# A decode layer's cached attention: PV in four column tiles, looped batches, part of wo early, and w4 in groups of four rows

## The chip, the cores and the metric

The kernel runs on one core of one Trainium2 chip. The metric is the device time of one execution in microseconds (us), taken as the median of several runs. The profile is one further execution with the hardware profiler on. Its span is just under 2 us shorter than the measured time of the same execution; spans are therefore compared with spans and times with times.

All runs are on a single core, so there is no second die to compare with. A run counts as fast unless it is more than 1.5% above the fastest run of its own kernel.

## The reference

One decode step for 8 sequences. A layer norm, a query projection (`wq`, 4 MB), attention of 32 heads over the last 2048 positions of a cache with 8 key/value head groups, an output projection (`wo`, 4 MB), a residual, then an MLP block whose token-shift branch is identically zero at a sequence length of 1 (so `w1` and `w2` are never read):

```python
def _A_ref(x, k_cache, v_cache, wq, wo):            # B=8, Sq=1, D=512, Hq=32, Hkv=8, Dh=128
    W = min(4096, max(256, Sk // 4))                # Sk = 8192, so W = 2048
    q = (x @ wq).reshape(B, Sq, Hq, Dh).transpose(0, 2, 1, 3)
    k = jnp.repeat(k_cache[:, :, Sk - W:, :], 4, axis=1)
    v = jnp.repeat(v_cache[:, :, Sk - W:, :], 4, axis=1)
    p = softmax(einsum("bhqd,bhkd->bhqk", q, k) * Dh ** -0.5)
    return einsum("bhqk,bhkd->bhqd", p, v).transpose(0, 2, 1, 3).reshape(B, Sq, Hq * Dh) @ wo

# ... B_ref: x1 = x + 0;  x1 + gelu(layernorm(x1) @ w3) @ w4,  F = 1792
h = x + _A_ref(layernorm(x), k_cache, v_cache, wq, wo)
return h + _B_ref(layernorm(h), w1, w2, w3, w4)
```

Everything is bf16. Keys and values are 64 MiB (67.1 MB), and the weights that are read bring the total to 79.2 MB.

## The kernel before

The kernel streams keys and values through SBUF slots of 2 MB. A slot holds four of the eight head groups of one sequence: two K slots and two V slots per sequence ("batch" below). All big loads go through one queue, issued by SyncE. The order of loads and the slots:

```python
NS = 10                                             # slots of 2 MB; wq lies in the last two
WO_CUT = [0, 16, 24, 28, 32]                        # wo in four loads: 2, 1, 0.5, 0.5 MB
W4_CUT = [0, 8, 12, 14]                             # w4 in three loads
early = NTILE - 2
order = [("k", t) for t in range(4)] + [("v", 0), ("v", 1), ("k", 4), ("v", early), ("k", 5)]
for t in range(2, NTILE - 4):
    order += [("v", t), ("k", t + 4)]
order += [("v", t) for t in range(NTILE - 4, NTILE) if t != early]
order += [("wo", 0), ("wo", 1), ("w3", 0), ("w4", 0)]
# ... free_slot(kind, t): SyncE waits for the transposes (k) or the PV (v) that emptied the slot
# ... w4 is loaded with two of its rows side by side: j=2, a run of 2 KB
w4_rows = B_w4.rearrange("(c p j) n -> p c (j n)", p=128, j=2)
```

TensorE (PE) first transposes K in pieces of 128x128, ScalarE and VectorE copy the result out of PSUM, and QK runs from there. After the softmax, P is transposed and PV runs with the probabilities as weights. Before the change PV used two column tiles of 64 columns and 512 result columns, and the result came out spread over four column blocks that VectorE had to add up:

```python
def pe_PV(e, v, parts=(0, 1)):
    b, gq = divmod(v, 2)
    # ... waits for the V slot and for the transposed probabilities
    vq = slots[:, slot, :].rearrange("p (q c d) -> p c q d", q=NT, d=DH)
    for cc in range(CC):                            # CC = 16
        a = cc % 2
        ins = e.matmul(pv_ps[gq][64 * a:64 * (a + 1), :].rearrange("p (q d) -> p q d", d=DH),
                       pT_sb[:, gq, cc, :], vq[:, cc, :, :],
                       start=(cc < 2), stop=(cc >= CC - 2), tile_position=(0, 64 * a), ...)

def dve_O1(e, v):                                   # 1 + 3 dependent VectorE operations per head group
    w = mrl[:, b % 2, gq, :]
    ins = e.tensor_scalar(o_sum[:, gq, :], pv_ps[gq][:, 0:DH], w[:, 0:1], None, ALU.mult)
    for q in range(1, NT):
        chain(e, ins, "dve_self", dve_self)
        ins = e.scalar_tensor_tensor(o_sum[:, gq, :], pv_ps[gq][:, q * DH:(q + 1) * DH], w[:, q:q + 1],
                                     o_sum[:, gq, :], ALU.mult, ALU.add)
```

In this kernel the stages of three batches are interleaved; the first batch and the last one stand outside PE's loop. At the end come the projection with `wo` (128 weight loads and matmuls), two norms, `w3` (56), gelu and `w4` (56, in four column tiles). `w3`'s columns are read as PE weights with a stride of 2, to match the two rows of `w4` that lie side by side.

## Time and profile before

| | before |
|---|---|
| time, median of 3 runs | 193.39 us (193.34 to 193.59) |
| span of the profiled run | 191.5 us |
| load queue, share of 16 DMA engines | 97.5% |
| PE / VectorE (DVE) / ScalarE (ACT) busy | 145.9 / 105.2 / 90.3 us |
| steady load rate | 431 GB/s |
| one batch: 8.39 MB at 431 GB/s | 19.46 us |

The end of the chain of waits of the kernel before (start, duration, what):

```profile
166.46 21.54 DMA slots<-in_B_w_dram
...
188.04 0.60 PE b L887 x16
...
188.68 0.41 PE b L887 x8
```

The chain is the wait for the last `w4` load, then 24 matmuls, a cast and the output. The compute before it had been waiting for data, not the reverse.

PE's timeline of the kernel before, one line of a steady batch and then the tail (start, duration, what, and in brackets the idle time before it with its releaser):

```profile
102.93 1.92 PE L595 MATMUL misc<-slots,pT_sb 128*64 128x512 bf16 x16
...
178.06 3.57 PE L796 MATMUL S_ps<-opl,slots 128*128 128x8 bf16 x128
...
184.34 1.66 PE L857 MATMUL misc<-uT,slots 128*128 128x8 bf16 x56 [1.52 <-DVE uT L833]
...
186.82 1.02 PE L887 MATMUL b<-slots,gT 128*8 128x128 bf16 x32 [0.51 <-DMA slots<-in_B_w_dram]
188.04 1.02 PE L887 MATMUL b<-slots,gT 128*8 128x128 bf16 x24 [0.20 <-DMA slots<-in_B_w_dram]
```

PV takes 1.92 us per head group of four (16 matmuls). The projection runs 178.06 to 181.63; the last group, of `w4`, waits twice for its load.

### The profile page before, as it was taken

Reading aid. Unit: us, or ns where it says so; the run is one execution under the profiler, and the core shown is the slowest. Engines: PE = TensorE matmul, PEld = TensorE weight load, DVE = VectorE, ACT = ScalarE, POOL = GpSimd, SP = SyncE. Lnnn points to the kernel's source line nnn. Section 1 sums busy time; section 2 is a strip of 40 time slices with the busy share of each in tenths; the row PEclk is TensorE's granted clock in tenths of the full one; section 3 lists DMA queues with packets and bytes.
Section 4 is the critical chain, followed back from the end, with each engine's and each line's share of the span. In section 5 each row is a group of like instructions: output and inputs, shape, how many; then the busy total and the mean of one; then the engine's idle time right before and its main releaser. Section 6 shows DMA issues by size and latency. Waiting matters only on the chain. (4 is left out here: it accounts for less than half of the span.)

```text
span 191.5 us, 4850 instructions
## 1 busy us (share of the span) xinstructions
PE 145.9 (76%) x2028; PEld 99.3 (52%) x2028; DVE 105.2 (55%) x287; ACT 90.3 (47%) x113; POOL 1.9 (1%) x14
## 2 busy tenths in 40 slices
PE   2027998796899869886989688968896888776854
PEld 0003876582857455645564547553655465343842
DVE  6401757464268474747474747565665657585141
ACT  3301676862656265536643564447344835406041
POOL 4000000000000000000000000000000000000000
PEclk9999999999699999999999999999999999999555
DMA  6999999999999999999999999999999999999991
GB/s 221 438 431 428 428 421 431 433 431 424 431 428 428 435 431 438 431 428 431 426 428 438 431 435 430 428 431 428 428 438 431 431 431 431 431 431 401 418 398 54
DMA packets 6857, 79.31 MB, mean 414 GB/s; under 512 B 688, under 2 KB 704, under 8 KB 2368
## 3 DMA queue, kind: packets, MB, share of 16 engines
q1 hardware_dynamic: 6832, 79.18, 97.5%
q8 instruction: 6, 0.10, 0.2%
q14 instruction: 3, 0.02, 0.0%
q10 hardware_dynamic: 16, 0.01, 0.0%
HBM read 79.18 MB, written 0.01 MB: 414 GB/s over the span
## 5 line engine op out<-in xcount | busy, mean ns | idle before, releaser
L496 ACT ACTIVATE kT_sb<-kT_ps 128x1024 bf16<-128x1024 bf16 x64 | 64.6, 1028 | 67.3 <-PE kT_ps L473 66.9
L473 PE MATMUL kT_ps<-perm_b,slots 128*128 128x128 bf16 x1024 | 68.5, 223 | 22.9 <-PEq L454 22.8
L473 PEld LDWEIGHTS kT_ps<-perm_b,slots 128*128 128x128 bf16 x1024 | 60.8, 100 | 33.7 <-issue 33.7
L500 DVE COPY kT_sb<-kT_ps 128x1024 bf16<-128x1024 bf16 x64 | 43.3, 688 | 27.1 <-PE kT_ps L473 27.1
L516 PE MATMUL S_ps<-kT_sb,qcur 128*32 128x512 bf16 x256 | 22.5, 387 | 0.8 <-PEq L454 0.8
L546 ACT ACTIVATE P_sb<-S_ps,mtile 128x1024 bf16<-128x1024 f32 x16 | 17.8, 1115 | 2.6 <-DVE mtile L537 2.5
L595 PE MATMUL b<-slots,pT_sb 128*64 128x512 bf16 x128 | 16.5, 384 | 1.2 <-PEq L454 1.2
L577 DVE TENSOR_TENSOR pT_sb<-kT_ps,maskT 128x1024 bf16<-128x1024 bf16 x16 | 10.5, 685 | 10.7 <-PE kT_ps L489 10.7
L595 PE MATMUL misc<-slots,pT_sb 128*64 128x512 bf16 x128 | 15.3, 382 | 0.6 <-PEq L454 0.6
L526 DVE TENSOR_REDUCE mtile<-S_ps 128x1 f32<-128x512 f32 x8 | 5.5, 692 | 13.6 <-PE S_ps L516 13.6
L595 PEld LDWEIGHTS misc<-slots,pT_sb 128*64 128x64 bf16 x128 | 6.8, 109 | 8.4 <-issue 3.6
L595 PEld LDWEIGHTS b<-slots,pT_sb 128*64 128x64 bf16 x128 | 6.2, 109 | 9.2 <-issue 5.7
L516 PEld LDWEIGHTS S_ps<-kT_sb,qcur 128*32 128x32 bf16 x256 | 5.3, 93 | 8.3 <-issue 4.2
L489 PEld LDWEIGHTS kT_ps<-ident_b,P_sb 128*128 128x128 bf16 x128 | 7.2, 98 | 4.1 <-issue 4.1
L489 PE MATMUL kT_ps<-ident_b,P_sb 128*128 128x128 bf16 x128 | 8.7, 219 | 0.6 <-PEq L454 0.6
L611 DVE SCALAR_TENSOR_TENSOR o_sum<-b,mrl,o_sum 128x128 f32<-128x128 f32 x24 | 8.4, 351 | 0.8
L611 DVE SCALAR_TENSOR_TENSOR o_sum<-misc,mrl,o_sum 128x128 f32<-128x128 f32 x24 | 8.4, 351 | 0.8
L395 PE MATMUL S_ps<-slots,xlnT 128*8 128x512 bf16 x32 | 3.6, 626 | 5.7 <-DMA slots<-in_A_wq_dram 5.7
L412 DVE TENSOR_SCALAR q_sb<-S_ps 128x512 bf16<-128x512 f32 x1 | 0.7, 692 | 9.1 <-PE S_ps L395 9.1
L626 DVE CAST o_all<-misc 16x128 bf16<-16x128 f32 x7 | 2.0, 279 | 6.4 <-PE misc L620 6.3
L395 PEld LDWEIGHTS S_ps<-slots,xlnT 128*8 128x8 bf16 x32 | 1.0, 117 | 7.4 <-issue 7.4
L657 ACT ACTIVATE opl<-kT_ps 128x224 bf16<-128x224 f32 x1 | 1.2, 1182 | 6.6 <-PE kT_ps L649 6.6
(104 smaller groups left out, 82.5 us busy)
## 6 DMA issues: line engine op xcount, KB each, us to landing
slots<-in_A_k_cache_dram SPq DMA_DIRECT2D x16, 2048.0 KB, 14.2
slots<-in_A_v_cache_dram SPq DMA_DIRECT2D x16, 2048.0 KB, 16.5
slots<-in_A_wq_dram SPq DMA_DIRECT2D x1, 4096.0 KB, 12.3
slots<-in_A_wo_dram SPq DMA_DIRECT2D x1, 2048.0 KB, 30.7
slots<-in_B_w_dram SPq DMA_DIRECT2D x2, 896.0 KB, 32.0
slots<-in_A_wo_dram SPq DMA_DIRECT2D x1, 1024.0 KB, 32.5
slots<-in_A_wo_dram SPq DMA_DIRECT2D x2, 512.0 KB, 33.7
slots<-in_B_w_dram SPq DMA_DIRECT2D x1, 1024.0 KB, 25.7
```

The costliest lines, as they stand in the source:

```text
L395: ins = e.matmul(S_ps[32 * j:32 * j + B, k, :], xlnT[:, kc * B:(kc + 1) * B], wq_v[:, kc, n0:n0 + 512], start=(kc == 0), stop=(kc == KC - ...
L473: ins = e.matmul(kT_ps[t % 2][:, c * 128:(c + 1) * 128], src[:, c * 128:(c + 1) * 128], perm_b[:, :], is_transpose=True)
L489: ins = e.matmul(kT_ps[half][:, c * 128:(c + 1) * 128], P_sb[:, half * W // 2 + c * 128:half * W // 2 + (c + 1) * 128], ident_b[:, :], is_ ...
L496: e.activation(kT_sb[:, i % NKT, 0:W // 2], kT_ps[i % 2][:, 0:W // 2], ACT.Copy).then_inc(sem_Elo, 1)
L500: e.tensor_copy(kT_sb[:, i % NKT, W // 2:W], kT_ps[i % 2][:, W // 2:W]).then_inc(sem_Ehi, 1)
L516: ins = e.matmul(S_ps[32 * gl:32 * (gl + 1), 0, :], qcur[:, GL * gq + gl, o:o + 32], kv[:, gl, :, :], start=(t == 0), stop=(t == 2 * NT - ...
L526: ins = e.tensor_reduce(mtile[:, 2, 0:1], S_ps[:, 0, :], AX.X, ALU.max)
L546: e.activation(P_sb[:, half * W // 2:(half + 1) * W // 2].rearrange("r (k g) -> r k g", g=GL), s_rep, ACT.Exp, bias=mtile[:, j, 0:1], scal ...
L577: e.tensor_tensor(pT_sb[:, :, half * hc:(half + 1) * hc, :].rearrange("p a c (g x) -> p (c g) a x", g=GL), kT_ps[half][:, 0:W // 2].rearra ...
L595: ins = e.matmul(pv_ps[gq][64 * a:64 * (a + 1), :].rearrange("p (q d) -> p q d", d=DH), pT_sb[:, gq, cc, :], vq[:, cc, :, :], start=(cc < ...
L611: ins = e.scalar_tensor_tensor(o_sum[:, gq, :], pv_ps[gq][:, q * DH:(q + 1) * DH], w[:, q:q + 1], o_sum[:, gq, :], ALU.mult, ALU.add)
L626: e.tensor_copy(o_all[:, gq, b, :], pv_ps[gq][0:GL * R, OT]).then_inc(sem_oT, 1)
```

## The change

The intent: make the compute of a batch shorter and simpler (PV yields one 128-column result in place of four blocks to be added), keep only two K and two V slots and put all eight batches into one loop, free enough SBUF to load a quarter of `wo` early, and give `wo` and `w4` longer runs per packet. The diff, cut to its core:

```diff
-NS = 10
+NS = 9
-        P_sb = sb([128, CC * 128], ...)      pT_sb = sb([128, 2, CC, 64], ...)
+        P_sb = sb([128, W], ...)             pT_sb = sb([128, CT, NT, 48], ...)
 # ... POOL now also clears P_sb and pT_sb at the start
+            e.memset(P_sb[:], 0.0).then_inc(sem_exp, 2)
+            e.memset(pT_sb[:], 0.0).then_inc(sem_pool, 1)
-        WO_CUT = [0, 16, 24, 28, 32]
+        WO_CUT = [0, 8, 24, 32]
-        order = [("k", t) for t in range(4)] + [("v", 0), ("v", 1), ("k", 4), ("v", early), ("k", 5)]
 # ... (the order shown above)
+        order = [("k", 0), ("k", 1), ("vl", 0), ("wo", 0)]
+        for b in range(NB - 1):
+            order += [("k", 2 * b + 2), ("k", 2 * b + 3), ("v", 2 * b), ("v", 2 * b + 1)]
+        order += [("vl", 1), ("wo", 1), ("wo", 2), ("w3", 0), ("w4", 0)]
 # ... w4: four rows side by side (4 KB runs) for 12 of 14 chunks, two for the rest
-                    w4_rows = B_w4.rearrange("(c p j) n -> p c (j n)", p=128, j=2)
+                        j = min(4, c1 - c0)
+                                    B_w4[c0 * 128:c1 * 128, :].rearrange("(c p j) n -> p c (j n)", p=128, j=j)
 # ... PV: 64 matmuls of 128 columns in four column tiles, both head groups into one PSUM area
+        def pe_PV(e, slot, gq, cs=range(CT)):
+            for c in cs:
+                for q in range(NT):
+                    k = q * CT + c
+                    ins = e.matmul(pv_ps[32 * q:32 * (q + 1), :], pT_sb[:, c, q, 16 * gq:16 * gq + 32],
+                                   slots[:, slot, k * DH:(k + 1) * DH], start=(gq == 0 and c == 0),
+                                   stop=(gq == 1 and c == CT - 1), tile_position=(0, 32 * q), ...)
 # ... one VectorE operation per batch in place of eight
+            e.tensor_scalar(o_sum[:, :], pv_ps, rL[:, :], None, ALU.mult).then_inc(sem_O1, 1)
 # ... PE: one loop over all 8 batches; PV of the batch before sits at its end
-            pe_block(e, 0)
-            with e.Fori(1, NB):
+            with nc.Fori(0, NB, engines=(mybir.EngineType.PE,), head_slot={mybir.EngineType.PE: 0}):
                 pe_block(e, 1, later_on)
 # ... w3's columns as PE weights: stride 4 (2 for the last two chunks) in place of 2
+        def w3_col(kc, fc):
+            j = 4 if fc < W4_CUT[2] else W4_CUT[3] - W4_CUT[2]
+            c0 = fc // 4 * 4
+            return w3_sb[:, kc, c0 * 128:(c0 + j) * 128].rearrange("r (p j) -> r j p", j=j)[:, fc - c0, :]
```

"vl" are the two V loads of the last batch; they have slots of their own, and the first of them comes third in the queue.

## The prediction

> **What bounds it now.** The load queue: the DMA part of the page gives it 97.5% of 16 engines' span, and the 40-slice table shows 421 to 438 GB/s from the second slice to the 35th. [...] this trace has 431 (stretches, 25 to 165 us). A batch brings 8.39 MB, so 19.5 us. PE is busy 16.4 us of every 20. 79.3 MB at 431 GB/s is 184 of the 191.5 us; the rest is the start (about 2.3 us lost in slice 1), the weights (392 to 423 GB/s from 174 to 186 us, under 1 us lost) and 3 us after the last weight. The chain of waits ends in that load, 24 matmuls, a cast and the output.
>
> **What the change does.**
> 1. Same bytes, same start, same end after the last weight. Only DMA rate, a starved queue, or a tail whose compute passes the weights can move the time.
> 2. PV: 16 matmuls of 512 columns in two column tiles (1.92 us per head group, timeline) become 64 of 128 columns in four. The closest shape, w4's matmuls in four tiles, took 1.02 us for 32, about 25 ns each after latency; estimate 1.7 to 1.9 us. No gain.
> 3. DVE drops six combining ops per batch (351 ns each) and two copies, off the critical path.
> 4. Only two K and two V slots stay, plus two for the last V. My estimate of one batch on PE, from timeline durations (transposes with eviction and P inside 10 us, last QK 0.9, PV 3.6, sum and placing 1, loop 0.5), is 16.3 us against 19.5 of DMA. A K slot frees about 5 us after landing and is needed after 14.6. At the start K slot 0 frees at about 24 us, with loads queued until 30; slot 1 at 31, needed by 34.5. The queue should never run dry.
> 5. Tail: 3 MB of wo instead of 4 follow the last V, which lands 2.4 us later, but fewer steps follow. I expect the projection to end at 179.8 us (181.6 before). Then w3 and w4 bind, as before.
> 6. Packets: w4 goes mostly from 2 to 4 KB, wo's last MB from 4 to 8 KB. If w4 ran at w3's rate (420 instead of 402 GB/s), 0.2 us; wo 0.1.
>
> **Prediction: 193.1 us**, 80% range 192.3 to 194.4. Faster by over 2%: 0.03; within 2%: 0.92; slower by over 2%: 0.05.
>
> **What would show it.** (1) DMA share 97 to 98%, slices at about 430 GB/s. (2) PV 1.7 to 1.9 us per head group. (3) DVE busy falls from 105 to about 90 us. (4) PE waits 2 to 3 us per batch for K and V loads. (5) The chain ends in the last w4 load, with wo's projection ended before 180.5 us. (6) The weights' slices rise to 410 to 425 GB/s.
>
> **What would make it wrong.** PE needs over 19.5 us per batch[...]: slots free late and each batch costs the excess. Or the longer loop body (some 640 instructions, estimated) stalls at its back jump; [...] this trace shows no gap there. Or the tail's compute passes the weights.

## More of the kernel before

The page of the kernel before. The first line is the span. "PE ... PEld ..." is busy time, share of the span and instruction count of each engine (PEld is PE's weight load). PEclk and GB/s give one value for each of 40 equal slices of the span: the clock granted to PE in tenths, and what the DMA engines moved. Then the chain of waits by source, and the two groups of PV's matmuls (busy time, mean ns of one, idle time before).

```profile
span 191.5 us, 4850 instructions
...
PE 145.9 (76%) x2028; PEld 99.3 (52%) x2028; DVE 105.2 (55%) x287; ACT 90.3 (47%) x113; POOL 1.9 (1%) x14
...
PEclk9999999999699999999999999999999999999555
...
GB/s 221 438 431 428 428 421 431 433 431 424 431 428 428 435 431 438 431 428 431 426 428 438 431 435 430 428 431 428 428 438 431 431 431 431 431 431 401 418 398 54
...
DMA slots<-in_B_w_dram 11%; SPq L291 3%; PE kT_ps L473 1%; PE b L887 1%; DVEq L911 0%; DVE xln_b L898 0%
...
L595 PE MATMUL b<-slots,pT_sb 128*64 128x512 bf16 x128 | 16.5, 384 | 1.2 <-PEq L454 1.2
...
L595 PE MATMUL misc<-slots,pT_sb 128*64 128x512 bf16 x128 | 15.3, 382 | 0.6 <-PEq L454 0.6
```

## The result, and the profile after

| | before | changed |
|---|---|---|
| time, median of 4 runs, timed together | 193.37 us (193.17 to 193.59) | 193.17 us (192.98 to 193.32) |
| span of the profiled run | 191.5 us | 191.2 us |
| load queue, share | 97.5% | 97.4% |
| PE / DVE / ACT busy | 145.9 / 105.2 / 90.3 us | 144.3 / 85.8 / 93.3 us |
| packets | 6857 | 6329 |
| PV per head group of four | 1.92 us | about 1.0 us |
| projection with `wo` ends at | 181.63 us | 181.67 us |
| last `w4` load seen by PE at | 188.68 us | 188.44 us |

The ratio is 0.9989, with a 95% interval of 0.9972 to 1.0006: the same. Ratios here and below are the mean time of one kernel's fast runs over that of the other's of the same rounds, so not quite the ratio of the medians that are quoted.

The same lines of the changed kernel's page, with the transposes in addition:

```profile
span 191.2 us, 6348 instructions
...
PE 144.3 (75%) x2848; PEld 117.7 (62%) x2848; DVE 85.8 (45%) x183; ACT 93.3 (49%) x119; POOL 6.4 (3%) x17
...
PEclk9999999589996997599879996999999969999555
...
GB/s 221 439 432 432 428 415 442 422 432 432 432 430 428 432 435 427 432 432 428 432 425 435 432 432 432 428 435 428 428 435 432 432 432 428 435 425 418 409 413 52
...
DMA slots<-in_B_w_dram 15%; PE kT_ps L438 3%; SPq L265 1%; PE b L761 1%; DVEq L785 0%; DVE xln_b L772 0%
...
L438 PE MATMUL kT_ps<-perm_b,slots 128*128 128x128 bf16 x1024 | 75.4, 238 | 15.6 <-PEq L421 15.4
...
L535 PE MATMUL misc<-slots,pT_sb 128*32 128x128 bf16 x1024 | 16.1, 219 | 0.9 <-PEq L421 0.9
```

Nearly everything that PE and VectorE do is different, and the GB/s line is the same. That is the whole result in two lines: VectorE lost 19 us of work and the queue didn't notice. The busy time of PV on PE halved (16.5 + 15.3 us to 16.1), the transposes went up to 75.4 us. The PEclk line explains the second: the granted clock now drops in several slices, mostly after a wait, and a transpose at a lower clock is counted longer: in the changed kernel's trace the transposes start 107 ns apart (median) in the stretches with a granted clock of 0.50, and 56 ns apart where it is 1.00. The mean clock over the run fell from 0.956 to 0.89. More waiting isn't the reason: between 40 and 160 us PE is idle for 19.4 us, and was for 20.1 before. Among the kernels with the new order the mean clock in this stretch goes with the waits for K: 0.91 here with 9.7 us of them, 0.95 with 5.5 us (pv2, below), 1.00 with none (pv1). But the kernel before has 0.99 with all its idle time, which is cut differently (23 waits of 0.2 to 2.3 us, most of them under 1 us). What makes the clock drop isn't shown. So PE's busy share stays nearly the same: of the 15.7 us that PV saves, 6.9 us come back in the slower transposes and some 5.6 us in smaller steps that the new order made longer (the transposes of P, the row sums and the placing of the result).

PE's timeline of the changed kernel, a steady batch and the tail:

```profile
108.65 1.97 PE L535 MATMUL misc<-slots,pT_sb 128*32 128x128 bf16 x128
...
114.01 5.36 PE L438 MATMUL kT_ps<-perm_b,slots 128*128 128x128 bf16 x64 [1.72 <-PEq L421]
...
176.21 0.63 PE L668 MATMUL S_ps<-opl,slots 128*128 128x8 bf16 x18 [0.22 <-ACT opl L559]
178.58 3.09 PE L668 MATMUL S_ps<-opl,slots 128*128 128x8 bf16 x110 [1.75 <-issue]
...
184.40 1.98 PE L733 MATMUL misc<-uT,slots 128*128 128x8 bf16 x56 [1.52 <-DVE uT L705]
...
186.72 2.10 PE L761 MATMUL b<-slots,gT 128*8 128x128 bf16 x56
```

Three things are to be seen. First, 128 PV matmuls, which are both head groups of a batch, take 1.97 us, where one head group alone took 1.92 us before. Second, after that PE waits 1.72 us for the next K slot and then transposes at a reduced clock (64 pieces in 5.36 us at a mean granted clock of 0.68; other batches have 3.93 to 3.98 us). That is where the shorter PV goes. Third, in the tail there is a new hole: the projection does 18 matmuls, stops for 1.75 us with nothing that the profile shows to wait for ("issue"), and does the other 110. Before, all 128 ran in 3.57 us.

The end of the chain of waits of the changed kernel:

```profile
159.60 28.16 DMA slots<-in_B_w_dram
...
187.81 0.60 PE b L761 x12
...
188.44 0.41 PE b L761 x5
```

It is the same end as before, 0.24 us earlier. The DMA share of the chain rose from 11% to 15% only because `w4` was put into the queue 6.9 us earlier (159.60 against 166.46) and stood there longer.

At the start, two things moved. VectorE's first operations of both kernels, the building of two identity matrices; before:

```profile
1.32 0.87 DVE L310 TENSOR_SCALAR ident_f<-iota_f 128x128 f32<-128x128 f32 x1 [1.32 <-POOL iota_f L215]
```

and changed:

```profile
1.32 5.68 DVE L286 TENSOR_SCALAR ident_f<-iota_f 128x128 f32<-128x128 f32 x1 [1.32 <-POOL iota_f L207]
```

POOL clears more memory now (6.4 us busy against 1.9), and VectorE's small operation stands for 5.7 us beside it. What holds it for so long isn't shown by this trace alone, but the times fit the clears: it ends at 7.00 us, and the last of POOL's clears runs from 4.27 to 6.92 us. Experiment 11 tests it. It costs no time here, since `wq` lands only at 13.1 us in both kernels.

The other is the issue of loads. SyncE's timeline of the changed kernel:

```profile
1.19 1.31 SPq L246 DMA_DIRECT2D slots<-in_A_k_cache_dram  x2
2.55 0.60 SPq L246 DMA_DIRECT2D slots<-in_A_v_cache_dram  x1
...
22.15 8.00 SPq L246 DMA_DIRECT2D slots<-in_A_k_cache_dram  x2
```

Before, four K and two V loads stood in the queue from the start, and the next was issued only at 35.92 us. Now there are three such loads and a quarter of `wo`. The third K load is issued at 22.15 us and the fourth about 7.5 us later, while the queue has work until about 30. It holds, but with little to spare.

### The profile page after: what moved, and what is told of

Same layout as the page of the kernel before. It is cut to its first block, busy times and chain, and to the rows that moved or that the text cites. A ratio compares the mean times of both kernels' runs of the same rounds, so it can differ in the third digit from the quotient of the medians.

```text
span 191.2 us, 6348 instructions
## 1 busy us (share of the span) xinstructions
PE 144.3 (75%) x2848; PEld 117.7 (62%) x2848; DVE 85.8 (45%) x183; ACT 93.3 (49%) x119; POOL 6.4 (3%) x17
## 2 busy tenths in 40 slices
DMA packets 6329, 79.31 MB, mean 415 GB/s; under 512 B 672, under 2 KB 688, under 8 KB 1712
## 3 DMA queue, kind: packets, MB, share of 16 engines
q1 hardware_dynamic: 6304, 79.18, 97.4%
## 5 line engine op out<-in xcount | busy, mean ns | idle before, releaser
L438 PE MATMUL kT_ps<-perm_b,slots 128*128 128x128 bf16 x1024 | 75.4, 238 | 15.6 <-PEq L421 15.4
L438 PEld LDWEIGHTS kT_ps<-perm_b,slots 128*128 128x128 bf16 x1024 | 68.1, 108 | 25.9 <-issue 25.6
L503 ACT ACTIVATE P_sb<-S_ps,mtile 128x1024 bf16<-128x1024 f32 x16 | 17.7, 1109 | 19.4 <-DVE mtile L498 19.4
L535 PE MATMUL misc<-slots,pT_sb 128*32 128x128 bf16 x1024 | 16.1, 219 | 0.9 <-PEq L421 0.9
L535 PEld LDWEIGHTS misc<-slots,pT_sb 128*32 128x32 bf16 x1024 | 14.6, 97 | 2.2 <-issue 2.1
L525 DVE TENSOR_TENSOR pT_sb<-kT_ps,mask 128x1024 bf16<-128x1024 bf16 x18 | 12.4, 688 | 3.6 <-PE kT_ps L454 3.5
L454 PE MATMUL kT_ps<-perm_p,P_sb 128*128 128x128 bf16 x144 | 10.9, 218 | 3.4 <-PEq L421 3.3
L454 PEld LDWEIGHTS kT_ps<-perm_p,P_sb 128*128 128x128 bf16 x144 | 8.5, 97 | 5.2 <-issue 5.0
L554 PE MATMUL b<-o_sum,selw 128*128 128x32 f32 x56 | 7.3, 275 | 4.3 <-PEq L421 4.3
L554 PEld LDWEIGHTS b<-o_sum,selw 128*128 128x128 f32 x56 | 6.8, 191 | 5.3 <-issue 5.3
L286 DVE TENSOR_SCALAR ident_f<-iota_f 128x128 f32<-128x128 f32 x1 | 5.7, 5682 | 1.3 <-POOL iota_f L207 1.3
```

Source lines behind the costliest of these rows:

```text
L286: e.tensor_single_scalar(ident_f[:], iota_f[:], 0.0, ALU.is_equal)
L438: ins = e.matmul(kT_ps[t % 2][:, c * 128:(c + 1) * 128], src[:, c * 128:(c + 1) * 128], perm_b[:, :], is_transpose=True)
L454: ins = e.matmul(kT_ps[half][:, c * 128:(c + 1) * 128], P_sb[:, k * 128:(k + 1) * 128], perm_p[:, :], is_transpose=True)
L503: e.activation(P_sb[:, half * W // 2:(half + 1) * W // 2].rearrange("r (k g) -> r k g", g=GL), bass.AP(tensor=S_ps[:, :, :].tensor, offset ...
L525: e.tensor_tensor(bass.AP(tensor=pT_sb[:, :, :, :].tensor, offset=h0 * NT * 48, ap=[[CT * NT * 48, 128], [48, CT // 2 * NT], [32, 2], [1, ...
L535: ins = e.matmul(pv_ps[32 * q:32 * (q + 1), :], pT_sb[:, c, q, 16 * gq:16 * gq + 32], slots[:, slot, k * DH:(k + 1) * DH], start=(gq == 0 ...
```

## The experiments

The theory (A): loads bound the kernel from end to end, the change makes the compute of a batch shorter by some amount, and the queue hides all of it. The main rival (B): the changed compute would be no better or worse by itself, or the gain was real and was eaten by a new cost (the stop in the projection, the strided weights, the thinner start). Twelve kernels were run (two of them, again and shift24, are the changed kernel itself, see 9 and 12), each on one chip, with the kernel before timed in the same rounds.

### 1 and 2. Both kernels with most of the load taken away

K and V loads into a slot that has been filled once bring only a quarter of their bytes; the rest of the slot keeps the data of an earlier batch. The results are wrong. They passed the comparison all the same, so it isn't sensitive to this. All waits and all compute stay as they are.

```diff
 # in the changed kernel (the kernel before: the same, with use[kind, t] == 1)
-                    e.dma_start(slots[:, slot + gq, :], src).then_inc(sem[gq], 16)
+                    n = C * DH if kind == "vl" or b == 0 else C * DH // 4
+                    e.dma_start(slots[:, slot + gq, 0:n], src[:, :, 0:n]).then_inc(sem[gq], 16)
```

The changed kernel with short loads:

> The changed kernel with every K and V load into a slot that was filled before cut to a quarter of its bytes (wrong result on purpose): 36 MB instead of 79, 85 us of loading at the measured 431 GB/s, so compute must bound. Theory A (both kernels wait for the load queue and their compute chains are nearly equally long): from the trace one batch of the compute chain is 4.3 + 8.8 + 2.0 + 1.7 = 16.7 us, which gives about 169 us in all, 164 to 175. Rival B (the change made the compute much shorter, by the 20 us that VectorE lost and the halved columns of PV, and the load queue hides it): 155 us or less, and at least 10 us below the kernel before cut in the same way.

The kernel before with short loads:

> The kernel before with the same cut of its loads (wrong result on purpose, 40 MB). Theory A: compute-bound at 16 to 17.5 us per batch, 168 to 178 us in all, within 5 us of the changed kernel with the cut. Rival B: at least 10 us longer than the changed kernel with the cut.

Measured: the kernel before with short loads took 177.68 us (177.37 to 178.48; ratio 0.9196 [0.9167, 0.9226] to the kernel before). The changed one took 171.71, 171.94, 172.04 and 169.17 us; the first three are classed slow only because of the fourth, so no ratio is given for it. The profiled run of it is one of those three. I therefore rest on the batch period inside the traces, in stretches where both pages show the full clock (16 transposes in the midst of a batch take 1.05 to 1.07 us in both, as they do at a granted clock of 1.00 in the changed kernel with full loads): the changed kernel first, then the kernel before (PE's timeline, first transposes of two successive batches).

```profile
84.90 3.98 PE L439 MATMUL kT_ps<-perm_b,slots 128*128 128x128 bf16 x64
...
101.00 3.98 PE L439 MATMUL kT_ps<-perm_b,slots 128*128 128x128 bf16 x64
```

```profile
80.30 1.96 PE L474 MATMUL kT_ps<-perm_b,slots 128*128 128x128 bf16 x32
...
97.77 1.96 PE L474 MATMUL kT_ps<-perm_b,slots 128*128 128x128 bf16 x32
```

A batch of the changed kernel takes 16.10 us of compute (101.00 - 84.90; four successive periods agree to 0.01 us), one of the kernel before 17.47 us (97.77 - 80.30). Both are under the 19.46 us that its bytes take. So the change does make the compute faster, by 1.37 us or 8% per batch, and with full loads all of it lies under the queue. Against the quoted numbers both theories missed a little: the gain over the whole run is about 6 us by the medians and 8.5 us by the one fast run of the changed kernel (169.17 against 177.68), more than A allowed (5) and less than B asked for (10). Why that one run was 2.5 us faster than the other three stays open.

### 3 and 4. How much slower could PV be?

The order of the 128 PV matmuls is changed so that only two of the four column tiles take turns, or none do (one tile after another). Same matmuls, same data, right results.

```diff
 # pv2
-            for c in cs:
-                for q in range(NT):
+            for q0 in (0, 2):
+                for c, q in [(c, q0 + a) for c in cs for a in range(2)]:
 # pv1
-            for c in cs:
-                for q in range(NT):
+            for q in range(NT):
+                for c in cs:
```

Two tiles:

> The changed kernel with the same PV matmuls in another order: only two of the four column tiles take turns. Estimate: the pair of head groups goes from 1.97 us to 3.6 us, 1.6 more per batch. Theory A (each batch has about 1.7 us of waiting for K plus the time lost to the low clock): the wait takes it up, 193 to 194 us, same. Rival B (PV time counts directly): 8 x 1.6, 206 us.

One tile:

> The same matmuls, all of one column tile after another, so that no two tiles run side by side. Estimate: the pair takes 7 us or more (55 ns each, as the transposes), 5 more per batch. Theory A: what exceeds the spare time of about 2.8 us per batch is paid, so 2.2 us or more x 7 plus 5 at the end: 210 us or more, with slices of the load queue below 400 GB/s. If instead it stays below 196, the column tiles are worth nothing here.

Measured: two tiles 193.48 us (193.04 to 194.1; ratio 1.0013 [0.9985, 1.0041], the same); one tile 200.74 us (200.54 to 200.98; 1.0383 [1.0365, 1.04], slower). PE's timeline with two tiles taking turns:

```profile
89.16 3.14 PE L535 MATMUL misc<-slots,pT_sb 128*32 128x128 bf16 x128
```

and with one tile after another:

```profile
90.70 5.86 PE L535 MATMUL misc<-slots,pT_sb 128*32 128x128 bf16 x128
...
98.05 3.95 PE L438 MATMUL kT_ps<-perm_b,slots 128*128 128x128 bf16 x64
...
118.00 3.93 PE L438 MATMUL kT_ps<-perm_b,slots 128*128 128x128 bf16 x64
```

With two tiles PV of a batch takes 3.14 us (in some batches it comes in two parts of 1.76 us with a wait for V between them), so 1.17 us more and not the 1.6 that I had estimated. PE's wait for K over 40 to 160 us shrinks from 9.7 to 5.5 us: the longer PV comes out of PE's waits and not out of the time. With one tile PV takes 5.86 us, the wait for K is gone, and the batch period is 19.95 us (118.00 - 98.05): 16.10 plus 3.89 more PV is 19.99, so the sum closes. That is 0.5 us per batch over the queue's 19.46, and PV of the tail adds 3.0 us (5.02 against 2.07 us). I had expected at least 210 us. PV is cheaper in this order than I thought, and the spare time of a batch is 19.46 - 16.10 = 3.36 us.

This is the test that shows the margin from both sides: adding 1.2 us per batch is free, adding 3.9 us isn't. It also shows that four tiles side by side matter for PV itself: 5.86, 3.14 and 1.97 us for one, two and four.

### 5 and 6. w4 with shorter runs

> The changed kernel with w4 loaded as before, two rows (2 KB) to a descriptor, and w3's columns read with stride 2; the grouping of four rows alone is undone. Theory A (the 0.2 us that the change gained comes from larger packets of the weights): 0.1 to 0.2 us slower than the changed kernel, so 193.3 to 193.4, inside the noise of the interval. Rival: grouping does nothing (ratio as the changed kernel's 0.999) or costs by the strided columns (then this run is the faster one).

> The same part exaggerated: one row (1 KB) to a descriptor, 1792 packets instead of 512. Theory A: the step from 2 to 4 KB is small because the cost per packet is about 5 ns on one of 16 engines (estimate from 402 against 431 GB/s); 1280 packets more cost 0.4 to 0.6 us: 193.6 to 193.8, weights' slices visibly lower. Rival: no change at all, below 193.3.

```diff
-                        j = min(4, c1 - c0)
+                        j = 2                      # w4_rows1: 1
 # ... and in w3_col
-            j = 4 if fc < W4_CUT[2] else W4_CUT[3] - W4_CUT[2]
-            c0 = fc // 4 * 4
+            j = 2                                  # w4_rows1: 1
+            c0 = fc // j * j
```

Measured: 2 KB runs 193.63 us (193.32 to 193.97; ratio to the kernel before 1.0018 [1.0005, 1.0031]); 1 KB runs 194.10 us (193.36 to 195.42; 1.0032 [1.0011, 1.0054]). The rates of the three slices of weights were 416, 404, 401 GB/s with 2 KB against 418, 409, 413 with the change's 4 KB (402, 404, 319 with 1 KB, but that profiled run was the slowest of its six, 195.42 us, and lost part of its time elsewhere, see 9). The direction is the expected one, at most a few tenths of a us per step. The changed kernel itself, however, is found at a ratio of 1.0017 (below), so 2 KB and 4 KB aren't told apart by time. What is clear is the other side of the grouping: with stride 1 (w4_rows1) and with stride 2 (w4_rows2) the 56 matmuls of `w3` take 1.66 us, with stride 4 they take 1.98 us. So two rows side by side cost nothing here, and four do.

### 7 and 8. wo later, and all of wo early

> The changed kernel with all of wo after the last V, as before; the early quarter alone is undone. Theory A: the bytes ahead of the last wo piece, of w3 and of w4 are the same, so nothing that ends last moves: 193.1 to 193.3; the last V lands 2.4 us earlier and waits in its slot; the projection starts earlier and ends at the same 181.7 us. Rival B (the early quarter buys time at the end or keeps the queue full at the start): 0.5 to 2.4 us slower.

> The changed kernel with all 4 MB of wo before the second batch's K. Then only w3 and w4 (3.7 MB, 8.9 us) follow the last V, and the chain V, PV, sum, placing, projection, norms, w3, gelu, w4 ends last. Estimate from the trace: last V at about 179.6 us, PV 1.0, placing 2.1, projection 3.6, norms 2.6, w3 1.7, gelu 0.5, w4 2.1: ends at 193.2 instead of 188.9, so 197 to 198 us. If the time stays at 193, the tail has more room than I think.

```diff
 # wo_late
-        order = [("k", 0), ("k", 1), ("vl", 0), ("wo", 0)]
+        order = [("k", 0), ("k", 1), ("vl", 0)]
-        order += [("vl", 1), ("wo", 1), ("wo", 2), ("w3", 0), ("w4", 0)]
+        order += [("vl", 1), ("wo", 0), ("wo", 1), ("wo", 2), ("w3", 0), ("w4", 0)]
 # wo_all_early
-        order = [("k", 0), ("k", 1), ("vl", 0), ("wo", 0)]
+        order = [("k", 0), ("k", 1), ("vl", 0), ("wo", 0), ("wo", 1), ("wo", 2)]
-        order += [("vl", 1), ("wo", 1), ("wo", 2), ("w3", 0), ("w4", 0)]
+        order += [("vl", 1), ("w3", 0), ("w4", 0)]
```

Measured: late 193.25 us (192.93 to 194.55; ratio 1.0019 [0.9993, 1.0044], the same); all early 199.74 us (199.44 to 200.96; 1.0346 [1.0323, 1.037], slower). In the profile of the late version the last V comes earlier, PE then waits 0.88 and 0.51 us for pieces of `wo`, the projection ends at 180.74 us, and the run still ends in the `w4` load. The early quarter buys nothing and costs nothing.

With all of `wo` early the last V comes so late that the tail's compute no longer fits under the remaining loads. The end of its chain of waits:

```profile
183.04 0.61 PE S_ps L668 x18
183.65 1.80 issue
185.45 3.08 PE S_ps L668 x110
```

In this kernel the stop of 1.8 us lies on the chain that ended last. I had expected 197 to 198 us without it; the stop is about the size of the miss. So the stop is a real cost that the changed kernel hides under the `w4` load and this one pays.

### 9. The changed kernel again

> The changed kernel once more, unedited, as the control for the other runs of this call and for the grouping of w4. Expected: 193.0 to 193.3, ratio to the kernel before 0.998 to 1.000. If it lies above 1.000, the 0.2 us were never a gain.

Nothing is edited. Measured: 193.78 us median (194.21, 193.75, 194.41, 193.2, 193.81, 193.19), ratio 1.0017 [0.9998, 1.0035]. The 0.2 us by which the first four runs were faster don't come again; the sign is even turned. The spread of the changed kernel (1.2 us in these runs) is wider than that of the kernel before in the same rounds (193.15 to 193.53). What was different in the profiled run shows in stretches of 1 us at the end. "Again" first:

```profile
188.00:189.00 1.00, 0.91 (x32) 0.62 (x24) 0.00 (x0) 0.00 (x0) 0.00 (x0) 0.50 0.09 35
```

and the first profiled run of the changed kernel:

```profile
188.00:189.00 1.00, 0.79 (x24) 0.22 (x15) 0.12 (x1) 0.12 (x1) 0.00 (x0) 0.50 0.01 2
```

The last columns are clock, DMA share and GB/s. By 180 us the two queues had moved the same within 0.1 MB; then in "again" a few of the 16 DMA engines still have work between 188 and 189 us (0.09 of them on average, 0.01 in the other run), and the last group of `w4` starts about 1 us later. Two other profiled runs with these loads (w4_rows1 and shift24) lose time at the start as well. There, the 64 transposes that free the first K slot take 5.6 and 5.4 us in place of 4.1; their starts are 107 ns apart at first, where 56 ns is the pace at a granted clock of 1.00 and 107 ns that at 0.50 (both in the changed kernel's first trace), so they ran at about half of the full clock. The third K load is issued at 23.9 or 24.3 us in place of 22.15, the slice at 33.5 to 38.3 us shows 368 or 376 GB/s in place of 422, and the 0.3 MB that are missing at 40 us are still missing at 180 us. That is 0.7 us at 431 GB/s, of the 1.0 us (shift24) and 2.4 us (w4_rows1) by which these profiled runs are longer. In "again" and pv2 the third K load is issued at 23.5 us, and nothing is missing at 40 us. In the kernel before the queue holds six loads at that time, and its profile shows no such slice. This reading comes from traces of runs that happened to differ; I made no kernel that turns it on and off.

### 10. Still longer runs, with still wider strides

If runs of 4 KB help the load, 7 and 8 KB should help more; the price is a stride of 8 in `w3`'s weight columns and of 4 in the projection's.

> The changed kernel with the weights in still larger runs: w3 with two rows side by side (7 KB instead of 3.5), w4 in three pieces of eight, four and two rows (8, 4 and 2 KB); the features of the residual are then kept with stride 4. Theory A (only the load queue's bytes and packet cost count): the last weight lands 0.1 to 0.3 us earlier, 192.8 to 193.1, the weights' slices at 415 to 430 GB/s. Rival (strided weights and columns cost the tail as much): 193.1 to 193.5.

```diff
-                                    B_w3.rearrange("(k p) f -> p k f", k=KC)[:, k0:k1, :]).then_inc(sem_w3[i], 16)
+                                    B_w3.rearrange("(p k) f -> p k f", k=KC)[:, k0:k1, :]).then_inc(sem_w3[i], 16)
-                        j = min(4, c1 - c0)
+                        j = c1 - c0
 # ... and the columns of x, wo, w4 and the output taken with stride 4, those of w3 with stride up to 8
```

Measured: 194.83 us (194.06 to 195.91), ratio 1.0084 [1.0056, 1.0112]. It is the only attempt at a version better than both. At a threshold of 2% it counts as the same, but the interval lies clear of 1: it is 0.8% longer. PE's timeline:

```profile
178.79 3.83 PE L668 MATMUL S_ps<-opl,slots 128*128 128x8 bf16 x110 [1.66 <-issue]
...
185.33 2.85 PE L733 MATMUL misc<-uT,slots 128*128 128x8 bf16 x56 [1.52 <-DVE uT L705]
...
188.53 1.81 PE L761 MATMUL b<-slots,gT 128*8 128x128 bf16 x56
```

The loads did end earlier: the slices of weights are 416, 421 and 295 GB/s, where the lower third one means that little was left to load. But the same 110 matmuls of the projection now take 3.83 us in place of 3.09, and the 56 of `w3` 2.85 in place of 1.98. The last group no longer waits for `w4`. The tail's compute had some 0.5 us of slack (the last group takes 1.67 us uninterrupted in the kernel before with short loads; had it not waited in the changed kernel, it would have ended at 188.4 in place of 188.86), and 0.74 + 0.87 us used it up. The weight loads themselves, grouped by line, in the changed kernel and in this one (mean ns of one):

```profile
L733 PEld LDWEIGHTS misc<-uT,slots 128*128 128x128 bf16 x56 | 1.9, 116 | 1.7 <-DVE uT L705 1.7
```

```profile
L733 PEld LDWEIGHTS misc<-uT,slots 128*128 128x128 bf16 x56 | 2.8, 146 | 1.7 <-DVE uT L705 1.7
```

With stride 1 (w4_rows1) and with stride 2 (w4_rows2, and the kernel before) the mean is 104 ns. So the weight loads of `w3` took longer with the wider strides, 116 ns (stride 4, a few at 2) and 146 ns (up to 8) against 104, and the stage with them; the granted clock in it is 0.50 in the kernel before, in the changed kernel and in this one. Why a stride of 4 costs and one of 2 doesn't isn't shown.

### 11. POOL's clears after VectorE's constants

> The changed kernel with the two large clears of POOL (P and its transpose) held until VectorE has built its constants. The profile of the changed kernel shows VectorE's two identity builds at 5.7 and 5.6 us where they took 0.87 and 0.80 before, while POOL clears. If the clears hold them up: 0.8 to 0.9 us again, the normalized x ready near 7 us instead of 10.9, and (theory A, the first 4 MB of wq land at 13 us anyway) no change of the time, 193.0 to 193.3. Rival: the start matters, 1 to 3 us faster.

```diff
 # POOL, before the two big clears
+            e.wait_ge(sem_dveP, DVEP_IDENT)
```

Measured: 193.23 us (193.04 to 195.45), ratio 1.0029 [0.9992, 1.0066], the same. The first VectorE operation in its timeline:

```profile
1.32 1.30 DVE L287 TENSOR_SCALAR ident_f<-iota_f 128x128 f32<-128x128 f32 x1 [1.32 <-POOL iota_f L207]
```

It takes 1.30 us in place of 5.68 when the clears are held back, so they were what held it, and the norm of x starts 4.4 us earlier. The time doesn't move, since everything there waits for `wq`.

### 12. Where does the stop in the projection come from?

The stop comes after the projection's 18th matmul in every profile that has it, whatever the time, and lasts 1.6 to 1.8 us in most of them (0.40 us in pv2). One theory, a guess of mine: PE waits there for instructions that have not come yet. Two queues of the profile carry instructions, q8 (six packets, 0.10 MB on the page) and q14 (three, 0.02 MB). The DMA page of the changed kernel for 176.0 to 177.5 us:

```profile
q8 instruction: 1, 0.02, 3.9%
```

I first took a smaller packet, of q14, for the cause: it lands at 178.0 to 178.5 us in the changed kernel (stop 176.84 to 178.58), and at the end of the stop in the kernels with short loads, with all of `wo` early and with `wo` late. pv2 speaks against that: there the stop lasts only 0.40 us, and q14's packet lands a good 1 us after its end. PE's timeline of pv2:

```profile
178.92 2.94 PE L668 MATMUL S_ps<-opl,slots 128*128 128x8 bf16 x110 [0.40 <-issue]
```

q8's packet fits all fourteen traces. In the eleven that have the stop, it ends 1.3 to 1.5 us after that packet has landed (177.07 and 178.58 us in the changed kernel, 177.48 and 178.92 us in pv2). In the three without a stop (pv1, the kernel before, and the kernel before with short loads) the packet has landed 2.0 us or more before the projection starts. So in these traces the length of the stop goes with when this packet lands and when PE gets to the 18th matmul. Whose instructions the packet brings isn't shown.

If the place is set by a fixed number of instructions, then 24 more instructions ahead of the tail should move the stop to an earlier matmul:

> The changed kernel with 24 register moves ahead of the last batch's code on PE. Four kernels stop for 1.8 us after exactly 18 of the 128 projection matmuls, also where all of wo landed long before, and one packet of the instruction queue lands at the end of that stop. If it is a wait for the instruction stream at a fixed place in the program, the stop moves 24 instructions forward, to 6 matmuls into the projection (a matmul and its weight load are two instructions). If it is a wait for data, it stays at 18. The time stays within 0.2 us of the control either way, since the weights land last.

```diff
 # PE, right after the loop over the batches
+            pad_reg = e.alloc_register("pad_reg")
+            for _ in range(24):
+                e.reg_mov(pad_reg, 0)
```

Measured: 193.66 us (193.02 to 195.3), ratio 1.0023 [0.9991, 1.0055]. PE's timeline:

```profile
176.31 0.61 PE L671 MATMUL S_ps<-opl,slots 128*128 128x8 bf16 x18 [0.22 <-ACT opl L559]
178.49 3.08 PE L671 MATMUL S_ps<-opl,slots 128*128 128x8 bf16 x110 [1.57 <-issue]
```

The stop stayed at 18, but this tests nothing: the moves were not kept in the program. This kernel gives byte for byte the same program for PE (102,656 bytes), and for every other engine, as the changed kernel. So the run is one more run of the changed kernel, and the stop must be where it was. Whether 24 more instructions would move it has not been tested. The packet that lands 1.3 to 1.5 us before the end of each stop speaks for a wait for instructions; no kernel here turns it on and off. As a second control it is of use: with "again" it gives twelve runs of the changed kernel on one chip, from 193.02 to 195.3 us, at ratios of 1.0017 and 1.0023.

## Why the prediction was right, and where it wasn't

The time: predicted 193.1 us (192.3 to 194.4), measured 193.17. The class "same" was right for the reason given: the kernel is bound by its loads, and the change leaves their bytes, their start and their end alone. Point by point, with the prediction's numbers:

1. *Same bytes, start and end.* Right. The queue's share is 97.4% against 97.5% and the slices stay near 430 GB/s. Experiments 1 to 4 show it in both directions: less load makes either kernel faster at once, while 1.2 us more of PV per batch do nothing.
2. *PV 1.7 to 1.9 us per head group, "no gain".* The mis-sized step: it is about 1.0 us, a gain of 0.9 us per head group. I had scaled from `w4`'s four-tile matmuls, which run at half the clock at the end of the program (0.50), and took them for the pace at full clock: in the trace one round of the four tiles starts every 107 ns there and every 56 ns in PV, where the granted clock was 1.00. Each PV matmul takes 15.4 ns (1.97 us / 128). The error of 0.7 to 0.9 us per head group was harmless in the sum only because PV isn't on the chain.
3. *DVE from 105 to about 90 us.* It fell to 85.8, in spite of some 4 us spent beside POOL's clears, which I had not seen coming (81.7 with the clears held back, experiment 11).
4. *16.3 us of compute per batch against 19.5 of load; PE waits 2 to 3 us per batch.* The first number is right (16.10 us with the loads taken away). The waits for K are 1.6 us per batch (9.7 us over six batches), fewer than predicted: most of the rest of the 3.36 us of spare time goes into slower transposes at a lower clock, up to 1.4 us per batch. The slots freed at 22.15 and about 30 us, where I had estimated 24 and 31.
5. *Projection ended before 180.5 us, then the last w4 load.* The end of the chain is right; the projection's end is not: 181.67 us. The missing term is the stop of 1.75 us; without it the projection would have ended at 179.9, where I had forecast 179.8. I had named a stall of instructions as a danger at the loop's back jump; the traces show no such stop there (with short loads, where PE waits for no load, the first transposes of a batch start at 101.00 us and the last matmuls of the batch before are counted to 101.16), but one of 1.75 us in the straight code after the loop. It costs nothing in this kernel and about 1.8 us in the kernel with all of `wo` early. Undoing the early quarter of `wo` showed that this part of the change has no effect on the time.
6. *Weights' slices at 410 to 425 GB/s, worth 0.2 us.* The slices are 418, 409 and 413, and the last weight is there 0.24 us earlier in the profiled run. But the gain doesn't hold: the changed kernel run again is at a ratio of 1.0017, and its runs there scatter three times as widely as those of the kernel before (in the first four runs they did not). The prediction counted the packets and not the price of the stride: 0.32 us more in the `w3` stage, harmless as long as the tail has slack.

Of the three dangers named, none came true in the change: PE needs 16.1 and not over 19.5 us (pv1 is the kernel where it does), the back jump shows no stall, and the tail's compute doesn't pass the weights (in rows7k8k and wo_all_early it does). What stays open: whether the stop in the projection is a wait for instructions and what places it there, why some DMA engines finish late at the very end in some runs, and whether the late third K load is the whole cause of the wider scatter. No kernel tried beats the two.

## What to carry to other kernels

When one queue is busy from end to end (97.5% here), price a change by what it does to the queue, and measure the compute's spare time by cutting the loads in both kernels: an 8% shorter batch was real and worth nothing. A trial edit that leaves the built program as it was tests nothing, so compare the programs first. Scale a matmul's time only from a stretch at the same granted clock: here a round of four tiles started every 107 ns at 0.50 and every 56 ns at 1.00. A grouping of rows that lengthened the DMA packets was paid for here in strided weight loads (104 ns each with stride 1 and 2, 116 with stride 4, a few at 2, and 146 with stride up to 8), so check which of the two ends last before going further.
